# Storing the block-turned probabilities of sixteen heads in four quarters, and where their loads stand in the queue

## The chip, the core and the metric

The kernel runs on one core of a Trainium2 chip. A core has four engines that compute: TensorE (PE in the profile; PEld is its loading of weights), VectorE (DVE), ScalarE (ACT) and GpSimd (POOL). SyncE (SP) issues nearly all DMA transfers of this kernel, one after another: an issue that waits holds up every issue behind it. Each engine works through its own list of instructions in order; semaphores connect the lists. The metric is the device time of the whole program in microseconds (us), as the median of several runs.

## The reference

Three parts follow each other: a causal attention with a forget gate, then two feed-forward layers on its output.

```
scores = q k^T / 8 + (cum[i] - cum[j])     # cum: running sum of log f; causal mask; 4 batches x 8 heads, 576 x 64
attn   = softmax(scores);  x = attn v      # 2304 tokens x 512
x      = relu(x w_in)^2 w_out              # 512 -> 2048 -> 512
h      = x w2_in;  out = (h - tanh h) w2_out
```

## The kernel before

All operands of products are split into a high and a low part (fp32r), and a product is the sum of three: high by high, low by high, high by low.

The first feed-forward layer takes the 2304 tokens in 8 blocks of 288 (`j`), each in 16 iterations (`i`) over the 2048 inner features. One iteration has 12 products for `hp` (L168) and 12 for `yp` (L197). The attention of the 32 heads is laid between these products, because a block needs only the heads of its batch. Heads 0 to 15 have their probabilities transposed on TensorE. Heads 16 to 31, of which this text speaks, are done otherwise, mostly beside blocks 2 to 5 (64 iterations, about 250 to 526 us): VectorE turns each 32 x 32 block of the probabilities `P` in place (`turn`, the tile `T`), and what is left of the transposition, a move of whole 32-blocks between partitions, is a trip to DRAM and back. `put` (L573) stores `T` to `p_d` as one transfer of 1 MB, 128 rows of 8 KB; `get` (L576 to L579) loads it back into the tile `PTl` in four transfers of 256 KB. Load `b` reads only columns `512 b` to `512 b + 511` of `p_d`, and fills every fourth partition. Two DRAM tensors `p_d` are used in turn.

When all four loads have landed, `p_high` (ACT) rounds `PTl` into `PTh` in four pieces `c`, `p_low` (DVE) leaves the rest in `PTl`, and TensorE makes the output products `o_ps` (L608 and L613): `pv_begin` has the five products with the high part, `pv_end` the five with the low part and the corner of 64 x 64. The first of the high products needs piece 0 of `PTh`, and they go on as the pieces come.

What is done when for a head `k` is written in `plan_head`, in slots of half an iteration. Head `k` begins at slot `o = -4 + int(7.75 (k - 17))`. The scores, their minimum and exponential come at `o` to `o+3`; `p_high` of head `k-1` comes at `o+4`; `put(k)` at `o+5`; `pv_end(k-1)` at `o+6`, behind the products of that slot; the output of head `k-1` at `o+7` (`xt`, `xs`, and for each odd head the two stores `x_d<-xsh` and `x_d<-xs`, L497 and L498); `get(k)` at `o+7` too, written behind them. So a put comes about 6.75 slots ahead of the `p_high` that reads its data. `get` can't be issued before `put` has landed and before `pv_end` of the head before has read `PTl`. Behind the loads, SP issues the next head's `R` (L273) and `QB` (L275), and later its `VR` (L294); some issues of `xhl<-x_d` and `y_d<-yst` fall in between.

The order in which each engine takes its instructions is, from block 2 on, the order in which this program emits them; ahead of that a scheduler sets it, which concerns head 16 alone (`put(UT)`, `get(UT)` in `attention`). SP's transfers use eight semaphores in turn (DMAHW0 to DMAHW7), and a transfer waits for the one that had its semaphore before, if nothing has shown yet that it is done.

Of the kernel before, what the change touches and what calls it, by code (L numbers as in the profile page):

```python
# [9 lines left out]
F32 = mybir.dt.float32  # L10
# [34 lines left out]
}  # L45
FETCH = {6: 4, 7: 5, 8: 6}
SPLIT_A = {4: 0, 6: 1, 8: 2, 9: 3}
# [22 lines left out]
def kernel(  # L70
# [23 lines left out]
    p_d = [dram.tile([128, 2048], F32, name=f"p_d{a}") for a in range(2)]  # L94
# [10 lines left out]
    def by(name):  # L105
        return {"A": nc.scalar, "V": nc.vector, "P": nc.gpsimd, "S": nc.sync}[ENG[name]]

    def rounded(eng, out, in_):
        if eng is nc.scalar:
            eng.activation(out, in_, AF.Copy)  # L110
        elif eng is nc.gpsimd:
            eng.tensor_scalar(out, in_, 1.0, 1.0, ALU.mult, ALU.mult)
        else:
            eng.tensor_copy(out, in_)
# [92 lines left out]
    R, QA, QB, VR, VH, ST, XS, P, PT = {}, {}, {}, {}, {}, {}, {}, {}, {}  # L207
# [362 lines left out]
            nc.vector.transpose(T[:, 0:2, 2, 0], p[:, 512:576].rearrange("p (b j) -> p b j", b=2))  # L570

    def put(u):
        by("put").dma_start(p_d[u % 2], PT["t"].rearrange("p b a s j -> p (b a s j)"))  # L573

    def get(u):
        src = p_d[u % 2].rearrange("(q i) (b n) -> i q b n", q=4, b=4)  # L576
# [81 lines left out]
    def attention(u0):  # L658
        for p in range(u0 - 2, UT):
            for t in (1, 4, 3, 2):  # L660
                if p >= u0:
                    trans(p, t)
                    yield
                if u0 <= p + 1:
                    scores(p + 1, t)
                    if t == 1:
                        scores(p + 1, 0)
                    elif p + 1 == UT:
                        turn(t)
                    yield  # L670
                if t == 4 and p + 2 < NU:
                    prep(p + 2)
                if t == 3 and p >= u0:
                    prep_v(p)
                if t == 3 and u0 - 1 <= p:
                    load_v(p + 1)
            if p + 3 < NU:
                load(p + 3)
            if p >= u0:
                pv(p)  # L680
            if p + 1 == UT:
                turn(1)
                turn(0)
                put(UT)
                get(UT)
            if p >= u0:
                yield
# [32 lines left out]

    def p_high(c):
        s0 = LOW[c]
        rounded(by("pth"), PT["h"][:, :, c, s0:], PT["l"][:, :, c, s0:].bitcast(F32))

    def p_low(c):
        s0 = LOW[c]
# [27 lines left out]
    def plan(slot, f, *a, behind=False):  # L754
        PLAN.setdefault(slot, ([], []))[behind].append((f, a))

    def plan_head(k):
        o = START + int(PERIOD * (k - UT - 1))
        new, old = k < NU, k > UT
        if new:  # L760
            plan(o, s_products, k, 4, behind=True)
            plan(o + 1, s_min, k, 4)
            plan(o + 1, s_exp, k, 4)
            plan(o + 1, s_products, k, 3, behind=True)
            plan(o + 2, s_min, k, 3)
            plan(o + 2, s_exp, k, 3)
            plan(o + 2, s_products, k, 2, behind=True)
            plan(o + 2, s_products, k, 1, behind=True)
            plan(o + 3, s_min, k, 2)
            plan(o + 3, s_exp, k, 2)  # L770
            plan(o + 3, s_min, k, 1)
            plan(o + 3, s_min, k, 0)
            plan(o + 3, s_exp, k, 1)
            plan(o + 3, s_exp, k, 0)
            plan(o + 3, s_sum, k, 3, 5)
            plan(o + 3, s_norm, k, 4)
            plan(o + 3, s_norm, k, 3)
            plan(o + 4, turn, 4)
            plan(o + 4, s_sum, k, 0, 3)
            plan(o + 4, s_norm, k, 2)  # L780
            plan(o + 4, s_norm, k, 1)
            plan(o + 4, s_norm, k, 0)
            plan(o + 4, turn, 3)
        if old:
            plan(o + 4, p_high, 0)
            plan(o + 4, p_high, 1)
            plan(o + 4, p_high, 2)
            plan(o + 4, p_high, 3)
            plan(o + 4, p_low, 0)
            for c in (1, 2, 3):  # L790
                plan(o + 5, p_low, c)
            plan(o + 5, pv_begin, k - 1, behind=True)
            plan(o + 6, pv_end, k - 1, behind=True)
            plan(o + 7, lambda u: PV[u][2](), k - 1)
            plan(o + 7, lambda u: PV.pop(u)[3](), k - 1)
        if new:
            plan(o + 5, turn, 2)
            plan(o + 5, turn, 1)
            plan(o + 5, turn, 0)
            plan(o + 5, put, k)  # L800
            plan(o + 7, get, k)
        if k == UT + 1:
            plan(o, prep_v, UT)
        if k + 1 < NU:
            if k > UT + 1:
                plan(o, load, k + 1)
            plan(o + 5, prep_hi_qk, k + 1)
            plan(o + 6, prep_copy, k + 1)
            plan(o + 6, prep_low, k + 1)
        if new:  # L810
            plan(o + 4, load_v, k)
            plan(o + 8, prep_v, k)
# [284 lines left out]
    for k in range(UT + 1, NU + 1):  # L1097
        plan_head(k)
    for g in range(NB * NF + LAG):
        j, i = divmod(g, NF)  # L1100
# [243 lines left out]
    for n in range(NSTEP):  # L1344
        b, g = divmod(n, NG)
# [86 lines left out]
    for n in range(REST):  # L1432
        k, g = divmod(n, NG)
# [34 lines left out]
    t = 2 * NQ * NYB  # L1468
# [68 lines left out]
```

## Time and profile before

| what | value |
|---|---|
| median of 3 runs | 1015.05 us (1013.46 to 1015.98) |
| the profiled execution | 1016.53 us, of which its span is 1014.8 us |
| TensorE busy, share of the span | 987.8 us, 97% |
| DVE, ACT, POOL busy | 720.0, 618.0, 378.1 us |
| mean granted TensorE clock | 0.993 of full |
| DMA | 211.56 MB, mean 208 GB/s |

TensorE is busy nearly always, so the time is the time of its products plus what it waits. Busy time of a product includes waiting inside a row of products, so a row that takes longer than the same row elsewhere has waited too. Times in the rows below are from the span's start. The profiled execution took 1.5 us more than the median of the runs.

### The profile page before, as it was taken

The page shows a single profiled execution, that of the slowest core. Times are in us where ns is not written, and L with a number is a line of the kernel's source. Part 1 is how long each engine was busy: PE and PEld are TensorE (multiplying, and loading weights), DVE is VectorE, ACT ScalarE, POOL GpSimd, SP SyncE. Part 2 cuts the span into 40 slices and gives each one's busy share as a digit, 9 for nine tenths or more (in the row PEclk, how much of TensorE's full clock was granted, in tenths as well). Part 3 has the DMA queues.
Part 4 walks back from the last instruction along what each step waited for, and adds up shares of the span by engine and source line. Part 5 has one row for each costly group of instructions (what it writes and reads, how often), then busy time and mean ns, then how long its engine had stood idle before and what let it go on. Part 6 is the DMA issues. An engine that isn't in the chain of part 4 may idle for free.

```text
span 1014.8 us, 19913 instructions
## 1 busy us (share of the span) xinstructions
PE 987.8 (97%) x7144; PEld 932.4 (92%) x7144; DVE 720.0 (71%) x1715; ACT 618.0 (61%) x1387; POOL 378.1 (37%) x452
## 2 busy tenths in 40 slices
PE   7989999999999999999999999999999999999998
PEld 7767778888999898999999999988999999999998
DVE  5899775776676777776735668578778788877851
ACT  4888776666777667677756777446556553333330
POOL 3343565455544323344303457146566420000000
PEclk8999999999999999999999999999999999999999
DMA  8646552213557556566547974987776699434451
GB/s 262 246 127 216 161 172 61 99 66 120 205 215 249 180 203 216 208 227 215 189 167 260 359 268 170 392 344 233 294 270 257 232 342 344 147 118 138 137 167 63
DMA packets 84531, 211.56 MB, mean 208 GB/s; under 512 B 8440, under 2 KB 33072, under 8 KB 80080
## 3 DMA queue, kind: packets, MB, share of 16 engines
q1 hardware_dynamic: 84304, 210.28, 59.4%
q8 instruction: 56, 0.92, 0.4%
q14 instruction: 43, 0.35, 0.1%
q10 hardware_dynamic: 128, 0.01, 0.0%
HBM read 132.20 MB, written 78.05 MB: 207 GB/s over the span
## 4 chain that ended last, share of the span: by engine, by line
PE 80%; DVE 6%; DMA 6%; ACT 4%; issue 2%; SPq 1%; POOL 1%; DVEq 0%; ACTq 0%; POOLq 0%
PE yp L197 17%; PE hp L168 17%; PE wp L1278 16%; PE wp L1202 12%; PE o_ps L608 5%; PE wp L1290 2%; PE o_ps L414 2%; DMA g_d<-gq 2%; DMA PTl<-p_d 2%; PE s_ps L373 1%; DVE wt L972 1%; PE s_ps L701 1%; PE s_ps L700 1%; PE t_ps L395 1%; PE t_ps L549 1%
## 5 line engine op out<-in xcount | busy, mean ns | idle before, releaser
L168 PE MATMUL hp<-xhl,w 128*128 128x288 f32 x1536 | 235.5, 299 | 2.8 <-ACT xhl L110 1.6
L168 PEld LDWEIGHTS hp<-xhl,w 128*128 128x128 f32 x1536 | 213.6, 189 | 5.9 <-ACT xhl L110 1.8
L197 PE MATMUL yp<-gh,w 128*128 128x288 f32 x1024 | 212.5, 299 | 0.0
L197 PEld LDWEIGHTS yp<-gh,w 128*128 128x128 f32 x1024 | 164.5, 188 | 1.9 <-issue 1.3
L1202 PE MATMUL wp<-xo,wg 128*128 128x288 f32 x1152 | 160.4, 296 | 4.2 <-DVE gq L1209 3.3
L1278 PE MATMUL wp<-go,wg 128*128 128x256 f32 x1344 | 161.4, 283 | 0.0
L1278 PEld LDWEIGHTS wp<-go,wg 128*128 128x128 f32 x1344 | 161.4, 192 | 0.0
L1202 PEld LDWEIGHTS wp<-xo,wg 128*128 128x128 f32 x1152 | 154.9, 188 | 6.4 <-DVE gq L1209 5.4
L197 PE MATMUL yp<-gl,w 128*128 128x288 f32 x512 | 151.9, 297 | 0.6 <-POOL gl L123 0.6
L525 POOL TENSOR_SCALAR P<-P,ST 128x192 f32<-128x192 f32 (+4 forms) x120 | 80.0, 675 | 135.6 <-DVE ST L716 79.9
L110 ACT ACTIVATE go<-gt 128x1792 fp32r<-128x1792 f32 (+1 forms) x34 | 58.3, 1717 | 101.1 <-PE wp L1278 86.4
L514 ACT ACTIVATE P<-P,ST 128x320 f32<-128x320 f32 (+4 forms) x151 | 84.8, 563 | 40.1 <-DVE ST L505 39.5
L505 DVE CUSTOM_DVE_ANT_0 P<-s_ps,mk 128x320 f32<-128x320 f32 (+3 forms) x151 | 63.3, 437 | 63.0 <-PE s_ps L701 28.2
L197 PEld LDWEIGHTS yp<-gl,w 128*128 128x128 f32 x512 | 96.5, 188 | 1.2 <-POOL gl L123 0.8
L123 DVE TENSOR_TENSOR gl<-tmp,gh 128x288 fp32r<-128x288 f32 x96 | 58.7, 613 | 53.2 <-ACT tmp L178 52.8
L123 DVE TENSOR_TENSOR go<-gt,go 128x1792 fp32r<-128x1792 f32 (+1 forms) x34 | 69.6, 2048 | 35.2 <-ACT go L110 32.3
L174 ACT ACTIVATE tmp<-hp 128x288 f32<-128x288 f32 x128 | 51.8, 405 | 56.4 <-PE hp L168 53.3
L123 POOL TENSOR_TENSOR wt<-wt,whi 128x512 f32<-128x512 f32 (+1 forms) x48 | 60.5, 1282 | 59.2 <-ACT whi L110 29.1
L178 ACT ACTIVATE tmp<-tmp 128x288 f32<-128x288 f32 x128 | 56.7, 443 | 3.3
L177 ACT ACTIVATE gh<-tmp 128x288 fp32r<-128x288 f32 x128 | 56.1, 438 | 2.0
L1209 DVE TENSOR_TENSOR gq<-wp,sm 128x288 f32<-128x288 f32 x96 | 40.7, 453 | 17.8 <-ACT sm L1208 10.9
L123 DVE TENSOR_TENSOR PTl<-PTl,PTh 128x512 fp32r<-128x512 f32 x64 | 39.2, 665 | 19.8 <-ACT PTh L110 17.9
(167 smaller groups left out, 1721.1 us busy)
## 6 DMA issues: line engine op xcount, KB each, us to landing
wg<-wg_d SPq DMA_DIRECT2D x24, 896.0 KB
g_d<-gq SPq DMA_DIRECT2D x32, 576.0 KB
raw<-in_w_dram SPq DMA_DIRECT2D x16, 1024.0 KB
p_d<-T SPq DMA_DIRECT2D x16, 1024.0 KB
PTl<-p_d SPq DMA_DIRECT2D x64, 256.0 KB
raw<-in_w_dram SPq DMA_DIRECT2D x32, 512.0 KB
gt<-g_d SPq DMA_DIRECT2D x32, 512.0 KB
R<-in_qk_dram SPq DMA_DIRECT2D x24, 576.0 KB
```

The costliest lines, as they stand in the source:

```text
L110: eng.activation(out, in_, AF.Copy)
L123: eng.tensor_tensor(out, in_, hi.bitcast(F32), ALU.subtract)
L168: nc.tensor.matmul(ps, w[:, k * 128:(k + 1) * 128], x[:, k], start=(jj == 0), stop=(jj == 11))
L174: nc.scalar.activation(tmp, ps, AF.Relu)
L177: nc.scalar.activation(gh, tmp, AF.Square)
L178: nc.scalar.activation(tmp, tmp, AF.Square)
L197: nc.tensor.matmul(yp[m][:, :n], w[:, c], x, start=(at == 0 and j == 0), stop=(at == NF - 1 and j == 2))
L505: nc.vector.tensor_tensor_reduce(p[:rows, a:b], ps[:rows, :b - a], mk[:rows, o:o + b - a], -0.125, 3.0e38 if mn is None else mn, ALU.add, ...
L514: nc.scalar.activation(p[:rows, :n], p[:rows, :n], AF.Exp, bias=mn, scale=-1.0, accum_out=st[:rows, 1, t:t + 1])
L525: by(n_by).tensor_scalar(p[:rows, :n], p[:rows, :n], st[:rows, 3, t:t + 1], 1.0, ALU.mult, ALU.mult)
L1202: nc.tensor.matmul(ps, wg[:, ws, k * 128:(k + 1) * 128], xo[:, xs, k], start=(i == 0 and first_), stop=(i == 5), skip_group_check=True)
L1278: nc.tensor.matmul(ps, wg[:, ws, m * 128:(m + 1) * 128], YO[n][xs][:, YX[xn]], start=(j == 0 and m == 0 and i == 0), stop=(j == 2 and i == ...
```

## The change

Three edits. `put` stores the four quarters `T[:, b]` as four transfers of 256 KB, 128 rows of 2 KB each, into the columns that load `b` reads. `get(k)` is planned at `o+6` behind the products, that is right behind `pv_end(k-1)`, where it was at `o+7` behind the output and its stores. `p_high` asks a new table entry `pth3` for the engine of piece 3; the entry is "A", as `pth` is.

```
-    "pth": "A", "ptl0": "V", ...
+    "pth": "A", "pth3": "A", "ptl0": "V", ...
...
     def put(u):
-        by("put").dma_start(p_d[u % 2], PT["t"].rearrange("p b a s j -> p (b a s j)"))
+        for b in range(4):
+            by("put").dma_start(p_d[u % 2][:, 512 * b:512 * b + 512], PT["t"][:, b].rearrange("p a s j -> p (a s j)"))
...
-        rounded(by("pth"), PT["h"][:, :, c, s0:], PT["l"][:, :, c, s0:].bitcast(F32))
+        rounded(by("pth3" if c == 3 else "pth"), PT["h"][:, :, c, s0:], PT["l"][:, :, c, s0:].bitcast(F32))
...
             plan(o + 5, put, k)
-            plan(o + 7, get, k)
+            plan(o + 6, get, k, behind=True)
```

Only SP's list changes; the lists of PE, DVE, ACT and POOL hold the same rows in the same order. The first place is SP's list for head 18, with the output of the odd head 17 behind it. Before (the names: `p_d_83` is one of the two DRAM tensors, `x_d_81` the attention output of one batch, DMAHW the semaphores of transfers):

```order
L573 DMA p_d_83<-T 128x2048 [waits DMAHW3_49,DVE_49]
L497 DMA x_d_81<-xsh 128x576 [waits DMAHW4_49,Activation_49]
L498 DMA x_d_81<-xs 128x576 [waits DMAHW5_49,Pool_49]
L579 DMA PTl<-p_d_83 32x4x512 [waits DMAHW6_49,DMAHW3_49,PE_49]
L579 DMA PTl<-p_d_83 32x4x512 [waits DMAHW7_49]
L579 DMA PTl<-p_d_83 32x4x512 [waits DMAHW0_49]
L579 DMA PTl<-p_d_83 32x4x512 [waits DMAHW1_49]
L273 DMA R<-in_qk_dram 128x1152 [waits DMAHW2_49]
L275 DMA QB<-aug_d 4x1152
```

The same place after the change:

```order
L574 DMA p_d_83<-T 128x512 [waits DMAHW1_49,DVE_49]
L574 DMA p_d_83<-T 128x512 [waits DMAHW2_49]
L574 DMA p_d_83<-T 128x512 [waits DMAHW3_49]
L574 DMA p_d_83<-T 128x512 [waits DMAHW4_49]
L580 DMA PTl<-p_d_83 32x4x512 [waits DMAHW5_49,DMAHW1_49,PE_49]
L580 DMA PTl<-p_d_83 32x4x512 [waits DMAHW6_49,DMAHW2_49]
L580 DMA PTl<-p_d_83 32x4x512 [waits DMAHW7_49,DMAHW3_49]
L580 DMA PTl<-p_d_83 32x4x512 [waits DMAHW4_49,DMAHW0_49]
L497 DMA x_d_81<-xsh 128x576 [waits Activation_49]
L498 DMA x_d_81<-xs 128x576 [waits Pool_49]
L273 DMA R<-in_qk_dram 128x1152
L275 DMA QB<-aug_d 4x1152
```

One store has become four; each load waits for the semaphore of its own quarter (the first for DMAHW1, the second for DMAHW2, and so on); and the loads have moved ahead of the two output stores. For the heads with no output stores behind them (17, 19, and so on) the loads stand where they stood, behind four puts instead of one.

The second place is SP's list for head 16, whose place the scheduler sets. Before (`VR` is the next head's v, `x_d_80` another batch's output):

```order
L573 DMA p_d_83<-T 128x2048 [waits DVE_49]
L294 DMA VR<-in_v_dram 128x1x320 [waits DMAHW5_49,Pool_49]
L497 DMA x_d_80<-xsh 128x576 [waits DMAHW1_49,Pool_49]
L498 DMA x_d_80<-xs 128x576 [waits DMAHW2_49,DVE_49,Pool_49]
L579 DMA PTl<-p_d_83 32x4x512 [waits DMAHW7_49,DMAHW3_49,PE_49]
```

After:

```order
L574 DMA p_d_83<-T 128x512 [waits DVE_49]
L574 DMA p_d_83<-T 128x512
L294 DMA VR<-in_v_dram 128x1x320 [waits DMAHW5_49,DMAHW1_49,Pool_49]
L497 DMA x_d_80<-xsh 128x576 [waits DMAHW2_49,Pool_49]
L498 DMA x_d_80<-xs 128x576 [waits DMAHW3_49,DVE_49,Pool_49]
L574 DMA p_d_83<-T 128x512 [waits DMAHW4_49]
L574 DMA p_d_83<-T 128x512
L580 DMA PTl<-p_d_83 32x4x512 [waits DMAHW7_49,DMAHW6_49,PE_49]
```

Here two of the four quarters stand behind the `VR` load and the two output stores.

## Rows read from the trace of the kernel before

**Rows 1.** Busy us of PE, PEld, DVE, ACT, POOL; clock; DMA share; GB/s

```profile
244.00:530.00 286.00, 281.57 (x2008) 269.41 (x2008) 197.27 (x552) 197.79 (x484) 108.25 (x135) 0.99 0.57 199
```

**Rows 2.** Waits, 244 to 530 us: total us, times, longest

```profile
ACT PTh L110 <- DMA PTl<-p_d: 18.8, 15, 3.3
...
PEld o_ps L608 <- ACT PTh L110: 7.1, 26, 0.6
...
PE o_ps L608 <- ACT PTh L110: 4.3, 4, 1.6
...
ACT PTh L110 <- DMA VR<-in_v_dram: 3.2, 1, 3.2
```

**Rows 3.** The same view for SP's queue, 244 to 530 us

```profile
SPq L579 <- DMA p_d<-T: 28.8, 9, 4.9
```

**Rows 4.** Timeline of SP: start us, duration us, issue, count

```profile
254.00 0.33 SPq L573 DMA_DIRECT2D p_d<-T  x1
...
257.20 0.32 SPq L498 DMA_DIRECT2D x_d<-xs  x1
258.27 2.56 SPq L579 DMA_DIRECT2D PTl<-p_d  x4
...
335.62 0.32 SPq L573 DMA_DIRECT2D p_d<-T  x1
340.88 2.52 SPq L579 DMA_DIRECT2D PTl<-p_d  x4
...
353.44 0.33 SPq L573 DMA_DIRECT2D p_d<-T  x1
...
359.38 2.54 SPq L579 DMA_DIRECT2D PTl<-p_d  x4
...
505.65 0.33 SPq L573 DMA_DIRECT2D p_d<-T  x1
509.62 2.55 SPq L579 DMA_DIRECT2D PTl<-p_d  x4
```

**Rows 5.** Timeline of ACT, the roundings into PTh; in brackets the idle before

```profile
264.90 2.09 ACT L110 ACTIVATE PTh<-PTl 128x512 fp32r<-128x512 f32 x4 [0.30 <-DMA PTl<-p_d]
...
349.09 2.09 ACT L110 ACTIVATE PTh<-PTl 128x512 fp32r<-128x512 f32 x4 [3.29 <-DMA PTl<-p_d]
...
515.76 2.09 ACT L110 ACTIVATE PTh<-PTl 128x512 fp32r<-128x512 f32 x4 [1.40 <-DMA PTl<-p_d]
```

**Rows 6.** Timeline of PE, the output products with the high part

```profile
267.40 0.98 PE L608 MATMUL o_ps<-PTh,VH 128*128 128x512 f32 x5
...
299.39 1.68 PE L608 MATMUL o_ps<-PTh,VH 128*128 128x512 f32 x5
...
349.86 1.81 PE L608 MATMUL o_ps<-PTh,VH 128*128 128x512 f32 x5 [1.65 <-ACT PTh L110]
...
402.82 1.64 PE L608 MATMUL o_ps<-PTh,VH 128*128 128x512 f32 x3 [1.62 <-ACT PTh L110]
...
420.46 1.81 PE L608 MATMUL o_ps<-PTh,VH 128*128 128x512 f32 x5 [0.62 <-ACT PTh L110]
```

**Rows 7.** Stretches of half a microsecond, columns as above

```profile
341.00:341.50 0.50, 0.50 (x6) 0.50 (x5) 0.36 (x1) 0.47 (x4) 0.00 (x0) 1.00 0.00 0
...
404.00:404.50 0.50, 0.50 (x2) 0.38 (x3) 0.50 (x2) 0.50 (x3) 0.00 (x0) 0.50 0.00 0
...
506.50:507.00 0.50, 0.50 (x5) 0.50 (x5) 0.00 (x0) 0.50 (x2) 0.00 (x0) 1.00 1.05 442
```

**Rows 8.** The chain that ended last: start us, duration us, products

```profile
404.87 2.64 PE hp L168 x12
...
436.27 1.60 PE hp L168 x12
...
441.44 1.68 PE hp L168 x12
...
457.88 1.66 PE hp L168 x12
```

2 rows, old and new, of the table ENG are left out of this document.

## The prediction, written before the changed kernel ran

> **What bounds the kernel now.** I read the engine totals of the stretch first, then the waits, then the timelines of SP, ACT and PE side by side, and last the chain of waits, to see what an unhindered period takes.
>
> Between 244 and 530 us TensorE is busy 281.57 of 286 us, and no other engine passes 198 [rows 1]. So time is gained here only where TensorE waits. The waits name one chain: ACT waits 18.8 us in 15 heads for the loads of `PTl` before it can round them into `PTh`, and 3.2 us in a sixteenth, which the view puts down to a `VR` load that landed last at that moment, though that rounding reads `PTl` [rows 2]; TensorE waits for those roundings, 4.3 us with nothing running and 7.1 us at weight loads inside the output products [rows 2]. That second wait hides in busy time: the five high products take 0.98 us where nothing is late and 1.68 or 1.81 us where they go at the pace of the roundings [rows 6].
>
> Item by item, TensorE's loss: head 21 (products at 349.86) 1.65 idle + 0.83 stretch = 2.48; head 24 (402.82) 1.62 + 0.83, and then a granted clock of half, 1.2 GHz, under which the next twelve products take 2.64 us where they take 1.60 to 1.68 at the full level, so 1.0 more [rows 6 to 8], 3.45 in all; head 25 (420.46) 0.62 + 0.83 = 1.45; eight more heads whose five products took 1.02 to 1.81 us, of which the one at 299.39 stands, together 3.54. Sum 10.9 us.
>
> A second way to the same number: from the group of twelve at 441.44 to that at 457.88 an undisturbed period of four iterations with one head takes 16.44 us [rows 8]. An iteration has two groups of twelve of 1.60, so the head's own products are 16.44 - 12.8 = 3.64. From the roundings of head 16 (264.90) to those of head 31 (515.76) [rows 5] there are 116 slots, 58 iterations, and 15 heads: 58 x 3.2 + 15 x 3.64 = 240.2, and it took 250.86. Loss 10.7 us. That is the most that earlier loads can give back; I use it.
>
> Why the loads are late: SP waits 28.8 us, nine times, for `put` to land [rows 3]. Undisturbed (head 31) the put is issued at t = 505.65, the first load at t + 3.97, the fourth about three quarters into the 2.55 us of the four issues, t + 5.9, and the roundings start at t + 10.11 [rows 4, 5]. Head 21 has its first load at t + 5.26, with the DMA engines at rest at 341 us [rows 4, 7]: what is lost is waiting for one transfer to end before the next begins, not bandwidth. Heads with output stores ahead of the loads have the first at t + 5.94 (353.44 to 359.38) [rows 4].
>
> **Part by part.** *Four stores.* Three more issues of 0.33 us on SP, which waits most of the time; nothing computes there. How soon a quarter lands no row shows. Bounds: a quarter of 3.97, 1.0 us after its issue, and the whole 3.97. 1.05 MB at the 442 GB/s of the put [rows 7] is 2.4 us, so 3.97 holds 1.6 us that doesn't go with bytes; a quarter alone would take 1.6 + 0.6 = 2.2. The first load can go at t + 2.2. The fourth quarter is issued at t + 1.0 and shares the engines with the others, so it lands at t + 4.0 if the bytes set it and at t + 5.0 if it needs the whole 3.97 behind its own issue. I take 4.0, nearest to the row of the whole put. So the fourth load, which the first rounding needs as well, goes at t + 4.0 to 5.0 and not at t + 5.9: 0.9 to 1.9 us sooner in an undisturbed head, 2.2 to 3.2 in head 21 (there it went at 340.88 + 1.9, t + 7.15).
>
> The Trainium skill (DMA: Bandwidth & Descriptors, section Bandwidth) speaks against it: batch transfers to 1 MiB or more. Its fit (Anatomy of one DMA, for the other descriptor path) is 2.0 us plus bytes over 436 GB/s: an estimate of 4.4 us for the whole store, where the trace has 3.97, and 2.6 for a quarter. By it the fourth quarter would land at t + 3.6 with the fixed parts side by side; with these behind each other it is the slow rival below.
>
> *The loads ahead of the output stores* (heads 18, 20, and so on to 30). Before, the fourth load went at t + 5.94 + 1.9 = t + 7.8; now at t + 4.0 to 5.0, 2.8 to 3.8 sooner. The two output stores, 0.59 MB, then fall into the loads' flight: at 442 GB/s up to 1.3 us back, leaving 1.5 to 2.5. What waits behind the loads: the two stores, then `R`, `QB` and `VR` of the next heads. The stores go when the fourth load has gone, about t + 4.6, where the second went just ahead of t + 5.9; `R` goes sooner than before. Nothing is late there. `pv_end` of the head before must be past as well; it stands one slot behind the put and is done about 1 us after it, so the quarters set the time.
>
> *Semaphores.* With three more transfers per head, the one eight places back is nearer: a `VR` load can now wait for the first load of its head. It stands behind all four loads, two stores, `R` and `QB`, when that load has about landed. Nothing.
>
> *Head 16.* Two of its quarters go behind `xs` (257.20), so at about 257.6 and 257.9 where the whole went at 254.00, and its last two loads at about 260 to 261.6 where the fourth went at 258.27 + 1.9 = 260.2 [rows 4]. Up to 1.4 us late. Cover: its roundings begin at 264.90, the first takes some 0.6 us, and TensorE comes at 267.40 with products of 0.98 us, so it hadn't waited [rows 5, 6]: 1.8 us of room. Without the cover it would cost those 1.4 us, once.
>
> *`pth3`.* The same engine; nothing.
>
> *What is late next.* In a head without loss ACT, DVE and TensorE meet with the 1.8 us of head 16 to spare, so no other engine takes over at once. I take what each head gains from TensorE's own loss: head 21 keeps 0 to 0.3; head 24, with output stores, 0 to 0.95 of its 2.45, and the half clock goes with the idle time; head 25 (no stores) 0 to 0.55; the smaller losses, all under 0.85, go. Kept 0 to 1.8, I take 0.9. Saved 10.7 - 0.9 = 9.8 us. The profiled execution took 1016.53 us, so 1006.7; it stood 1.5 above the median of the runs, so 1005.2 for a median.
>
> **Rivals.**
>
> *Company in the queue (half the gain).* The quarters fly while the first loads do. Should they delay them by all their own time, three quarters at 442 GB/s, 1.8 us, heads without stores gain nothing, and heads 18, 20, 22, 24, 26, 28, 30 keep theirs: 0.70 + 0.24 + 0.83 + 3.45 + 0.10 + 0.32 + 0.04 = 5.7 us, 1009.4. For it: head 21's loads took 8.2 us (340.88 to its roundings at 349.09) against 6.1 in head 31, which no load of a next head followed [rows 4, 5]. Against: the engines were at rest ahead of the loads [rows 7].
>
> *Hidden, or the wait turned into another.* Loads land sooner, but ACT comes to the rounding with its own work late, or DVE's low parts hold TensorE. Then about 1 us or nothing is saved, 1014 to 1015. Against: ACT stood idle right before the roundings in all sixteen heads [rows 2].
>
> *Slower: quarters behind each other.* Should the 1.6 us that don't go with bytes be paid four times in a row, the last quarter lands at t + 4 x 1.6 + 2.4 = t + 8.8. Loads without stores ahead then come 2.9 us later than t + 5.9, with them 1.0 later than t + 7.8. Eight heads lose up to 2.9 less about 1 us of room, seven up to 1.0: 8 x 1.9 + 7 x 0.5 = 19 us, 1034. It decides from the point where the last quarter lands later than t + 5.9; the skill's rule on batching is the sentence beside it. Against: four loads issued 0.63 us apart land 6.1 us after the first [rows 4, 5], so in the same queue fixed parts overlap.
>
> *It doesn't do what it says.* Should each load wait for the whole store, only the move ahead of the stores is left, about 5.7 us as in the first rival. The order shows a wait for its own quarter, so I give this little.
>
> **How the numbers follow.** Forecast 66% (1003 to 1008), company in the queue 18% and the whole store 2% (1008 to 1011.5), hidden 9% (1012 to 1016), slower 5% (1018 to 1034). A measurement of this kernel tells 0.3%, 3 us, from no change. So faster 0.87, the first three and a little of the hidden case; same 0.08; slower 0.05. The range runs from 1002, all 10.9 us saved and two more for the spread of runs (1013.46 to 1015.98), to 1011.5, the end of the second case; what it leaves out is hidden and slower.
>
> **What would show it.** The first of the four loads about 2 us behind the first store, the fourth 4 to 5 us behind it; in heads 18 to 30 the loads ahead of both output stores. ACT's wait for `PTl` falls from 22 us to under 5; the five high products at 0.97 to 1.1 us in nearly all heads; no half clock near 404 us; the stretch from the first roundings to the last 10 us shorter. It is wrong if the fourth load doesn't go earlier than t + 5.5, if the wait of TensorE for `PTh` stays above 5 us, or if the stretch shrinks and the time is given back behind 530 us.

## The result and the profile after

The changed kernel takes 1003.61 us (median of 4 runs, 1000.44 to 1004.88) where the kernel before took 1014.97 beside it: a ratio of 0.9885, with an interval of 0.9856 to 0.9913. Two later groups of runs of the same kernel gave 0.9895 (0.9857 to 0.9933) and 0.9900 (0.9880 to 0.9919). So it is faster by about 1%, 9.3 to 11.4 us between the medians of a group. The profiled execution took 1002.52 us, its span 1000.7.

Engine totals of 244 to 530 us, with the columns of [rows 1]:

```profile
244.00:530.00 286.00, 284.86 (x2092) 279.09 (x2090) 206.06 (x558) 202.78 (x499) 121.65 (x134) 1.00 0.61 207
```

TensorE is busy 284.86 us instead of 281.57, and in the same 286 us it did 2092 products instead of 2008. The window reaches further into the work than before, so the two counts are not of the same products. Idle time fell by 3.3 us; what more was gained was hidden in busy rows. The waits of that stretch, which answer to [rows 2]:

```profile
DVE PTl L123 <- ACT PTh L110: 4.6, 4, 3.2
...
ACT PTh L110 <- DMA PTl<-p_d: 1.3, 2, 0.9
...
PEld hp L168 <- DMA xhl<-x_d: 1.0, 1, 1.0
PE hp L168 <- DMA xhl<-x_d: 0.8, 1, 0.8
...
PEld o_ps L609 <- ACT PTh L110: 0.6, 1, 0.6
...
PE o_ps L609 <- ACT PTh L110: 0.4, 1, 0.4
```

ACT's wait for the loads has gone from 22 us to 1.3, TensorE's waits for the roundings from 4.3 and 7.1 us to 0.4 and 0.6. What is left of these stands at 248.78 us, in the products of head 15, whose probabilities take no trip to DRAM. New is one wait of TensorE for `xhl`, 0.8 us. SP's list around the heads 16 and 31 shows the change itself (answers to [rows 4]):

```profile
252.66 0.80 SPq L574 DMA_DIRECT2D p_d<-T  x2
...
256.22 0.90 SPq L574 DMA_DIRECT2D p_d<-T  x2
257.23 3.22 SPq L580 DMA_DIRECT2D PTl<-p_d  x4
260.50 1.06 SPq L891 DMA_DIRECT2D xhl<-x_d  x2
...
333.08 2.39 SPq L574 DMA_DIRECT2D p_d<-T  x4
335.68 2.80 SPq L580 DMA_DIRECT2D PTl<-p_d  x4
...
493.01 1.80 SPq L574 DMA_DIRECT2D p_d<-T  x4
495.28 2.64 SPq L580 DMA_DIRECT2D PTl<-p_d  x4
```

In head 31 the first load goes at t + 2.27 (t + 3.97 before) and the four issues end at t + 4.9 (t + 6.5 before); in head 21 the first load goes at t + 2.6 (t + 5.26 before). The output products of the heads that had waited, which answer to [rows 6]:

```profile
264.72 0.75 PE L168 MATMUL hp<-xhl,w 128*128 128x288 f32 x3 [0.77 <-DMA xhl<-x_d]
266.91 0.97 PE L609 MATMUL o_ps<-PTh,VH 128*128 128x512 f32 x5
...
345.81 0.97 PE L609 MATMUL o_ps<-PTh,VH 128*128 128x512 f32 x5
...
395.05 0.97 PE L609 MATMUL o_ps<-PTh,VH 128*128 128x512 f32 x5
...
410.04 0.97 PE L609 MATMUL o_ps<-PTh,VH 128*128 128x512 f32 x5
...
490.45 0.97 PE L609 MATMUL o_ps<-PTh,VH 128*128 128x512 f32 x5
505.21 0.97 PE L609 MATMUL o_ps<-PTh,VH 128*128 128x512 f32 x5
```

Heads 16, 21, 24, 25, 30 and 31: 0.97 us each and no idle time ahead, as in all sixteen (0.97 to 0.99). From head 16's products to head 31's it takes 505.21 - 266.91 = 238.30 us; before, 517.60 - 267.40 = 250.20, with this row for head 31:

```profile
517.60 0.97 PE L608 MATMUL o_ps<-PTh,VH 128*128 128x512 f32 x5
```

This distance, called the stretch below, holds the effect on the heads and is little disturbed by the rest of the program: 11.9 us less. The roundings, by which the prediction measured, moved together by 13.3 us (264.35 to 501.88, before 264.90 to 515.76); 1.5 of that is ACT coming earlier to head 31 than TensorE has use for (3.3 us ahead of the products, before 1.8). The half microseconds that answer to [rows 7]:

```profile
336.50:337.00 0.50, 0.50 (x6) 0.50 (x5) 0.25 (x2) 0.50 (x2) 0.00 (x0) 1.00 1.03 385
...
404.00:404.50 0.50, 0.50 (x6) 0.50 (x5) 0.28 (x2) 0.50 (x3) 0.00 (x0) 1.00 0.71 229
```

The DMA engines no longer rest between the store and the loads of head 21, and the clock near 404 us is full.

The two profiled executions differ by 14.0 us, more than the medians. Of that, 11.9 is the stretch, 0.5 lies ahead of it and 1.7 behind it (1014.8 - 517.6 = 497.2 us before, 1000.7 - 505.21 = 495.5 after). The part behind ran from 493.9 to 499.0 us in the profiles of the kernels below, which have the same work there, so I count no gain in it.

### The profile page after: what moved, and what is told of

The parts are those of the page before. It is cut to its first block, busy times and chain, and to the rows that moved or that the text cites. A ratio compares the mean times of both kernels' runs of the same rounds, so it can differ in the third digit from the quotient of the medians.

```text
span 1000.7 us, 19994 instructions
## 1 busy us (share of the span) xinstructions
PE 978.0 (98%) x7144; PEld 930.1 (93%) x7144; DVE 722.6 (72%) x1715; ACT 615.8 (62%) x1387; POOL 393.7 (39%) x452
## 4 chain that ended last, share of the span: by engine, by line
PE 82%; DVE 6%; DMA 5%; ACT 3%; issue 1%; POOL 1%; SPq 1%; DVEq 0%; POOLq 0%; ACTq 0%
PE yp L197 19%; PE hp L168 19%; PE wp L1279 16%; PE wp L1203 12%; PE o_ps L609 4%; PE wp L1291 2%; DMA g_d<-gq 2%; PE o_ps L414 2%; PE s_ps L373 1%; PE s_ps L702 1%; DVE wt L973 1%; PE s_ps L701 1%; PE t_ps L549 1%; DMA R<-in_qk_dram 1%; PE t_ps L395 1%
## 5 line engine op out<-in xcount | busy, mean ns | idle before, releaser
L525 POOL TENSOR_SCALAR P<-P,ST 128x192 f32<-128x192 f32 (+4 forms) x120 | 96.6, 812 | 134.7 <-DVE ST L717 79.3
L1210 DVE TENSOR_TENSOR gq<-wp,sm 128x288 f32<-128x288 f32 x96 | 40.7, 452 | 17.6 <-ACT sm L1209 10.7
L1341 POOL TENSOR_TENSOR gq<-sm,sm 128x288 f32<-128x288 f32 x32 | 28.6, 893 | 56.0 <-ACT sm L1340 34.8
```

The lines of the kernel that those rows point to most:

```text
L525: by(n_by).tensor_scalar(p[:rows, :n], p[:rows, :n], st[:rows, 3, t:t + 1], 1.0, ALU.mult, ALU.mult)
```

## The experiments

Theory A: what TensorE lost is the lateness of a head's loads and nothing else; the move gives it back to the heads whose loads stood behind output stores (18, 20, ... 30), the quarters to the others. Its rivals: one of the two parts does it all, or the quarters do it by landing sooner in themselves and not by overlapping with the loads. Each kernel ran in several rounds beside the kernel before, in three groups: the changed kernel, its two parts and head 16's store whole; the changed kernel and head 16's store whole once more; and the other four. Each run has one trace.

**The changed kernel again.** No edit.

> The changed kernel again, beside its parts. All theories: 0.9885 of the kernel before, 0.987 to 0.991; ACT's wait for the loads of PTl under 3 us, the stretch from the first high output products of head 16 to those of head 31 about 238 us (250.2 before).

Ratio 0.9895 (0.9857 to 0.9933), stretch 504.12 - 265.95 = 238.2, ACT's wait for the loads 1.4 us. As expected. The kernel before ran from 1007.2 to 1020.4 us in the 23 runs beside it, this one from 1001.8 to 1004.8.

**The quarters alone.**

```
-            plan(o + 6, get, k, behind=True)
+            plan(o + 7, get, k)
```

> Four stores, but the loads planned at o+7 behind the output stores, as before. Theory A (each head's loss is the lateness of its fourth load): heads 17, 21, 25, 29 have no stores ahead and gain their 5 to 6 us; heads 18 to 30 with stores have their first load at t + 5.9 as before and keep their losses. Less 0.8 us for the xhl wait behind head 16: ratio 0.9950 to 0.9960. Rival (the move ahead of the stores does it all, the quarters nothing): 1.000. Rival (the quarters do it all): 0.9885.

0.9961 (0.9933 to 0.9989). Stretch 513.75 - 269.55 = 244.2, so 6.0 of the 11.9 us. In its trace, the output products of heads 17, 22 and 25:

```profile
284.41 0.97 PE L609 MATMUL o_ps<-PTh,VH 128*128 128x512 f32 x5
...
366.28 1.81 PE L609 MATMUL o_ps<-PTh,VH 128*128 128x512 f32 x5
...
416.43 0.97 PE L609 MATMUL o_ps<-PTh,VH 128*128 128x512 f32 x5
```

Heads 17 and 25, without stores ahead, are cured; head 22 is not, and its loads went at t + 5.9 as before:

```profile
352.32 1.80 SPq L574 DMA_DIRECT2D p_d<-T  x4
...
358.24 2.56 SPq L580 DMA_DIRECT2D PTl<-p_d  x4
```

Heads 20, 22, 24, 26 and 28 lost time, as theory A has it (head 18 didn't, against it); head 21 kept 0.6 us. But the losses are not those of before: head 24 lost 1.1 us (0.23 idle, 1.81 for its products) where it had lost 2.7 before (the prediction's 2.45, see the loss below) and had the half clock behind it, and head 26 lost 1.65 (0.77 idle, 1.85) where it had lost 0.1. Neither rival's number; the ratio is just above the range of theory A, which its interval holds.

**The move alone.** The store is the one of 1 MB.

```
-        for b in range(4):
-            by("put").dma_start(p_d[u % 2][:, 512 * b:512 * b + 512], ...)
+        by("put").dma_start(p_d[u % 2], PT["t"].rearrange("p b a s j -> p (b a s j)"))
```

> One store of 1 MB, the loads right behind the last output product. Theory A: heads 18, 20, ... 30 have their first load at t + 4.0 instead of t + 5.9 and lose nothing but about 0.5 us in head 24; the heads without stores (17, 21, 25, 29) keep 5 to 6 us. Ratio 0.9940 to 0.9950; the two parts together give about the whole. Rival (the quarters do it all): 1.000. Rival (the parts overlap, either alone gives most): 0.990.

0.9948 (0.9924 to 0.9972). Stretch 509.11 - 266.00 = 243.1, so 7.1 of 11.9 us. Heads 21, 22 and 25 in its trace:

```profile
346.83 1.81 PE L608 MATMUL o_ps<-PTh,VH 128*128 128x512 f32 x5 [1.51 <-ACT PTh L110]
...
364.11 1.30 PE L608 MATMUL o_ps<-PTh,VH 128*128 128x512 f32 x5
...
412.91 1.81 PE L608 MATMUL o_ps<-PTh,VH 128*128 128x512 f32 x5 [0.37 <-ACT PTh L110]
```

Now 21 and 25 lose, and of the heads with stores only 22, a little. Its first load went at t + 4.6 and head 21's at t + 5.0 (332.30 to 337.28), where a store alone needs 3.97. Against theory A, heads 17 and 29, which have no stores ahead, took 1.04 and 1.12 us (1.70 and 1.57 before): the move nearly cured them too. The two parts give back 6.0 + 7.1 = 13.1 us, the whole 11.9. That the sums meet within 1.2 us is in part luck. Heads 17, 18 and 29 and most of 24 are cured, or nearly, by either part alone, and the half clock behind head 24, 1.0 us, is gone in both traces and so counted twice; against this stands the new loss of head 26 with the quarters alone. Heads 21 and 25 need the quarters and heads 20, 22 and 28 the move, as theory A has it; why 17, 18 and 29 need only one of the two no run shows.

**Loads that wait for no store.** A bound: heads 17 to 31 load the tensor of the head before, so the output isn't the reference's.

```
-        src = p_d[u % 2].rearrange("(q i) (b n) -> i q b n", q=4, b=4)
+        src = p_d[(u if u == UT else u + 1) % 2].rearrange("(q i) (b n) -> i q b n", q=4, b=4)
```

> The changed kernel, but for heads 17 to 31 the loads read the DRAM tensor of the head before, which landed long ago (the output products take that head's probabilities): the loads wait for no store, only for the last output product. First load about t + 1.9, right behind the four store issues, the fourth about t + 3.7. Theory A (with the quarters the fourth load is early enough everywhere): nothing left to gain, stretch of output products 238 to 239 us, ratio 0.987 to 0.991. Rival (the loads still cost something, hidden in the products): stretch under 237 us, ratio under 0.986.

0.9895 (0.9873 to 0.9918). Stretch 506.96 - 268.51 = 238.45, with the first load at t + 1.9 (350.02 to 351.91 in head 22). Loads that wait for nothing but the last output product gain nothing more: with the quarters, all that waiting for the stores had cost is given back.

**Halves.** Two stores of 512 KB.

```
-        for b in range(4):
+        for b in range(0, 4, 2):
-            by("put").dma_start(p_d[u % 2][:, 512 * b:512 * b + 512], PT["t"][:, b] ...)
+            by("put").dma_start(p_d[u % 2][:, 512 * b:512 * b + 1024], PT["t"][:, b:b + 2] ...)
```

> Two stores of 512 KB instead of four of 256 KB, the loads right behind the last output product. Theory A (only the fourth load's time counts): fourth load at about t + 4.5, as with quarters; stretch 238 to 240 us, ratio 0.988 to 0.991. Rival (finer is better, each early load counts): heads 21 and 25 keep about half their loss, stretch 240 to 241, ratio about 0.992.

0.9916 (0.9895 to 0.9938). Stretch 505.97 - 267.44 = 238.5, as with quarters; only head 21's products took longer than 0.99 (1.32 us). By the trace halves are nearly enough: head 25 keeps nothing, where the rival had half its loss. The time of 0.9916 lies nearer the rival's 0.992, though its interval holds both. Undecided.

**The last quarter's load first.** All four loads then stand behind the landing of the last quarter.

```
-        for b in range(4):
+        for b in (3, 0, 1, 2):
             dst = PT["l"][b::4] ...
```

> The changed kernel with the loads issued in the order 3, 0, 1, 2, so all four stand behind the last quarter's landing. First load at t + 4.0, last at t + 5.9 as in an undisturbed head of the kernel before. Theory A (the overlap of loads with stores is what the quarters bring): as with the whole store and the move alone, heads 21, 22, 25 and 29 lose again, stretch 241 to 243 us, ratio 0.993 to 0.995. Rival (smaller stores land sooner in themselves): stretch 238 to 239, ratio 0.989.

0.9944 (0.9920 to 0.9967). Stretch 507.66 - 266.36 = 241.3. The loads of head 22 go at t + 4.3 (348.86 to 353.20), head 21's at t + 4.9. Heads 21, 22 and 25:

```profile
345.38 1.70 PE L609 MATMUL o_ps<-PTh,VH 128*128 128x512 f32 x5
...
362.54 0.99 PE L609 MATMUL o_ps<-PTh,VH 128*128 128x512 f32 x5
...
410.87 1.81 PE L609 MATMUL o_ps<-PTh,VH 128*128 128x512 f32 x5 [0.32 <-ACT PTh L110]
```

21, 25 and 29 (1.70 us) lose again, as without quarters, with the same four stores; 22, which was expected to, doesn't. The four quarters together land no sooner than the one store; what they bring is that three loads are under way when the last lands. That is shown for 3.0 us of the 4.8 between the move alone (243.1) and the changed kernel (238.3). The other 1.8 stay won in this order too, and not by earlier loads: in head 21 the first goes at t + 4.88 against t + 4.98 in the move alone, but the roundings start at t + 11.96 against t + 13.76. The loads themselves took less time there, and no run shows why. The traced execution, 1004.72 us, was one of the faster ones of this kernel (median 1009.16), so its stretch shows rather less than the usual loss.

**Head 16's store whole.** The `xhl` wait at the start of block 2 is tested by taking away head 16's quarters alone.

```
     def put(u):
+        if u == UT:
+            by("put").dma_start(p_d[u % 2], PT["t"].rearrange("p b a s j -> p (b a s j)"))
+            return
         for b in range(4):
```

> The changed kernel, with head 16's store left whole, so that no quarter of it stands behind the output stores and the loads of xhl that block 2 begins with go out earlier. If TensorE's 0.8 us of waiting for xhl at the start of block 2 comes from those quarters: that wait gone, 0.5 to 1.0 us faster than the changed kernel (ratio 0.9878 where that has 0.9885). Rival (xhl is late for the output stores' sake, as before): no difference, the 0.8 us wait stays.

0.9885 (0.9845 to 0.9925), median 1002.60 where the changed kernel had 1003.96 in the same group. SP's list at head 16:

```profile
253.35 0.33 SPq L574 DMA_DIRECT2D p_d<-T  x1
...
257.62 2.57 SPq L583 DMA_DIRECT2D PTl<-p_d  x4
260.24 1.06 SPq L894 DMA_DIRECT2D xhl<-x_d  x2
```

and the first products of block 2:

```profile
263.30 2.12 PE L168 MATMUL hp<-xhl,w 128*128 128x288 f32 x12
```

The transfers of `xhl` go 6.9 us after the store, as before the change, where the changed kernel has 7.8 (252.66 to 260.50), and TensorE's idle time is gone: the twelve products take 2.12 us from first to last (1.97 in the kernel before), against 264.72 + 0.75 - 262.61 = 2.86 in the changed kernel (they begin with the nine at 262.61):

```profile
262.61 1.35 PE L168 MATMUL hp<-xhl,w 128*128 128x288 f32 x9
```

The stretch begins behind this place and doesn't hold it. The pair ran once more:

> The changed kernel once more, for a pair with the next: ratio 0.988 to 0.990.

> The changed kernel with head 16's store whole, once more: its trace is without the wait for xhl; if the 0.7 us are worth their time, its median is 0.5 to 1.5 us under the changed kernel's of the same call; if the spread of runs hides them, within 0.5 us.

0.9900 (0.9880 to 0.9919) and 0.9888 (0.9866 to 0.9909), medians 1004.49 and 1003.40. In both groups the version with head 16 whole is 1.1 to 1.4 us ahead, and TensorE's idle time for `xhl` (0.7 to 0.8 us) is in all three traces of the one and in neither of the other, though one of these has 0.2 us at a weight load. Other traces agree: with half of head 16's store behind the output stores (the kernel of halves) it is 0.4 us, with the whole store ahead of them (the move alone) 0.2. The intervals overlap, so the 0.7 us are shown by the trace, and by the times only likely. Its medians are the lowest of the versions that give the reference's output, by less than the intervals.

**Halves, head 16 whole.** Both edits together.

> Two stores for each head, head 16's store whole. If halves do as well as quarters and head 16's 0.7 us are saved: 0.988 to 0.989, stretch 238 to 240 us, no wait for xhl at the start of block 2. If halves are too coarse: 0.990 to 0.992.

0.9907 (0.9883 to 0.9930), stretch 503.31 - 264.23 = 239.1, no idle time for `xhl`. The ratio lies in the range for halves that are too coarse, the stretch in the other, and the interval holds both; nothing better than quarters. Head 21's products took 1.81 us here and 1.32 with halves above, where five traces with quarters have 0.97 to 1.40: what halves lose, they lose there.

## Why the prediction was right, point by point

*What bounds the kernel.* Right. TensorE waited for ACT, ACT for the loads, the loads for the end of the store and for the output stores; with the loads free of the store (old data) nothing more is gained. That part of the wait hid in busy rows was right too: 18.8 and 3.2 us of ACT's waiting went, and with them the rows of 1.68 and 1.81.

*The loss, 10.7 us.* Too small by 1.2: the stretch shrank by 11.9, to 238.3. The sum head by head (10.9) was nearer than the count by periods. That sum misread one row: head 24's in [rows 6] has only three of the five products. Whole, it adds 0.25 us to that head's loss:

```profile
402.82 2.05 PE L608 MATMUL o_ps<-PTh,VH 128*128 128x512 f32 x5 [1.62 <-ACT PTh L110]
```

Of the 11.9, 1.0 is the half clock, which the one trace of the kernel before has there and no trace of the other kernels; how many of its runs have it is not known. The count by periods failed in one place: it put 15 heads' scores and products into the distance from head 16 to head 31, but no new scores lie in the last of the fifteen periods (490.45 to 505.21 is 14.76 us for eight slots, where others take 16.4), so the unhindered distance is 1.6 us shorter than the 240.2 worked out: 238.6, near the 238.3 measured.

*Four stores.* The first load at t + 2.2: 2.27 in head 31. The fourth at t + 4.0 to 5.0: the four issues run from t + 2.27 to t + 4.9, so the last begins at about t + 4.3. Right, but for heads 19 and 24, where issues of `xhl` stand between the stores and the loads and the fourth went at about t + 5.4 and t + 5.3. Four issues in a row took 1.8 us of SP (2.3 and 2.4 in heads 20 and 21), not 1.3; SP waits anyway. The 442 GB/s were the rate of one half microsecond: the five of that put from 506.5 on moved 295 to 492, 403 in the mean, so about 1.4 us and not 1.6 don't go with bytes.

*What is kept, 0.9 us.* In this trace nothing was kept. Heads 21 and 24, for which I left 0.3 and 0.95, show 0.97 us and no idle time. The gain per head was too careful. It was taken from loads that are issued in 2.55 us, but in heads 24 and 25 the four issues had taken longer:

```profile
393.02 3.32 SPq L579 DMA_DIRECT2D PTl<-p_d  x4
...
410.33 3.54 SPq L579 DMA_DIRECT2D PTl<-p_d  x4
```

The roundings of heads 24 and 25 before, then of 21, 24 and 25 after:

```profile
402.05 2.08 ACT L110 ACTIVATE PTh<-PTl 128x512 fp32r<-128x512 f32 x4 [3.18 <-DMA VR<-in_v_dram]
...
419.69 2.08 ACT L110 ACTIVATE PTh<-PTl 128x512 fp32r<-128x512 f32 x4 [2.47 <-DMA PTl<-p_d]
```

```profile
343.93 2.09 ACT L110 ACTIVATE PTh<-PTl 128x512 fp32r<-128x512 f32 x4 [0.37 <-DMA PTl<-p_d]
...
392.91 2.09 ACT L110 ACTIVATE PTh<-PTl 128x512 fp32r<-128x512 f32 x4
...
407.61 2.09 ACT L110 ACTIVATE PTh<-PTl 128x512 fp32r<-128x512 f32 x4
```

Counted from the put (335.62, 387.18 and 406.40 before, 333.08, 380.93 and 397.50 after), they start 2.6, 2.9 and 3.2 us sooner in heads 21, 24 and 25; TensorE had lost 2.5, 2.7 and 1.5 there. So head 21 has hardly anything to spare, and the term was right to exist: in the last trace of the changed kernel (the pair's), SP took 3.01 us for head 21's four stores, its first load went at t + 3.24, and its products took longer.

```profile
331.20 3.01 SPq L574 DMA_DIRECT2D p_d<-T  x4
334.44 2.75 SPq L580 DMA_DIRECT2D PTl<-p_d  x4
```

```profile
343.94 1.40 PE L609 MATMUL o_ps<-PTh,VH 128*128 128x512 f32 x5
```

There the stretch is 239.2 us. The three traces of the changed kernel have 238.2 to 239.2, so 0 to 1 us is kept.

*Head 16, nothing.* Wrong: this is the step that failed. I asked who waits for its loads and found 1.8 us of cover (it held: 0.97 us at 266.91, no idle time). I did not ask what stands behind the loads on SP: the last parts of `xhl` for block 2, which went out 0.9 us later and cost TensorE 0.7 to 0.8 us. With the store whole they go out as before, and the idle time is gone.

*The half clock, the output stores, the semaphores, `pth3`.* The clock is full near 404 us. The output stores behind the loads hold up no row of TensorE, though SP waits 3.1 us for one of them to land ahead of an issue of `xhl` (0.2 before). Of the semaphores' former transfers I expected no wait; SP's waits have four, all for transfers of `xhl`, 2.3 us together where there were none. The two longest:

```profile
SPq L574 <- DMA xhl<-x_d: 1.0, 1, 1.0
SPq L275 <- DMA xhl<-x_d: 0.8, 1, 0.8
```

Neither a put (L574) nor the load of `QB` (L275) touches `xhl`, so these waits are for the semaphore. They fall where no store or load of `P` is due, and TensorE shows nothing of them. So the terms of nothing were right for the time, not for the queue.

*The rivals.* Company in the queue: head 21's loads take 335.68 to its roundings at 343.93, 8.2 us, as before; the quarters cost them nothing. Quarters behind each other: no, with the last quarter's load first it went at t + 4.28 in head 31, so all four overlap. Whole store: no, three loads are under way first. Hidden: no, the roundings came sooner and TensorE's rows shrank with them. The forecast of 1005.2 had 9.8 us; measured are 9.3 to 11.4 between medians, and the 11.9 of the stretch less the 0.8 of `xhl`, 11.1, lies in that. That the forecast came so near is in part luck: a loss 1.2 too small and 0.9 kept that this trace doesn't show stand against the 0.8 of `xhl` that it left out.

## What to carry to other kernels

A round trip through DRAM that waits for its whole store pays the store and the loads one after the other; cut the store as the loads are cut, and let each load wait for its own piece. But look at both ends of the queue: what the loads stood behind was worth as much here as the cutting, and what stands behind the loads pays if they go later. A loss can be counted from rows that stretch and from the length of a period; check that every period counted holds the same work.

## What the runs showed of the hardware

Four stores of 256 KB issued together land no sooner and hardly later than one of 1 MB: with all loads behind the last quarter the first load went at t + 4.28 in head 31 and t + 4.34 in head 22, with one store (the move alone) at t + 3.88 and t + 4.61. Their rows of 2 KB instead of 8 KB moved at 377 to 393 GB/s in five half microseconds of head 31, 383 in the mean, where the whole store had 403. One of the five:

```profile
495.00:495.50 0.50, 0.50 (x6) 0.50 (x5) 0.50 (x3) 0.50 (x2) 0.00 (x0) 1.00 1.02 377
```

Back to back, such issues took SP about 0.45 us each, where a single one takes 0.33; in heads 20 and 21 one of the four took 1.0 us, and no run shows why. The times scatter: the kernel before ran over 13 us in the 23 runs of one group and over 6 in the 14 and 11 of the others, the changed one over 3.0 and 4.5 in six runs each. That waits for transfers make them scatter is not shown.
